# An attention-plus-MLP kernel: normalized rows transposed by DMA instead of TensorE, with output stores and v loads moved to ScalarE's DMA queue

## Chip, cores and metric

The kernel runs on one core of one Trainium2 chip. The metric is device time in microseconds (us) of one execution; three executions of the kernel before gave 367.08, 367.95 and 368.9, so the median is 367.95.

## What is computed

For 8 batches, 8 heads, 576 positions and a head width of 64 the kernel computes a causal attention whose scores carry a bias from a running sum, and then a layer norm and a two-layer MLP with a residual on the 512 values of each position:

```python
scores = scale * np.matmul(q, k.transpose(0, 1, 3, 2))
cum = np.cumsum(np.maximum(s, 0.0), axis=-1)
bias = -(cum[:, :, :, None] - cum[:, :, None, :])
scores = np.where(causal, -1e9, scores + np.minimum(bias, 0.0))
attn = softmax(scores)                      # over the last axis
x = np.matmul(attn, v).transpose(0, 2, 1, 3).reshape(8, 576, 512)
xn = (x - mu) / np.sqrt(var + 1e-06) * g_ln
out = x + np.maximum(xn @ w_ch1, 0.0) @ w_ch2
```

## The kernel before, in words

Everything is written out by hand: one Python loop over the 64 heads, `n = 8*b + h` (L745), puts instructions into each engine's queue, and each engine runs its queue in order. `pre(n)` (L675) issues what head `n` needs from GpSimd and SyncE ahead of its matmuls. `scores(b, h)` (L304) makes three PSUM banks `sa`, `sb`, `sc` of transposed scores (three buffers, `ps_s`), which ScalarE turns into `er` by Exp (L323); from head 10 on GpSimd masks the diagonal blocks of `er` (L331). `scores_d` (L341) does the last 64 by 64 corner of two heads at once, into `sd`. `pv_next()` (L729) multiplies with `v` for the head two steps back (`pot`, L389), and VectorE divides into `xb` (a batch's rows, 4 tiles of 128 positions by 512) and `xm` (the last 64 positions of two batches together).

Between these, TensorE is filled with *units* of the MLP of the batch before, taken from `queue` by `run_units`. A batch has 32 units: 16 of `mlp1` (L493: four 128x512 matmuls into `ph`, a Relu into `hT` by ScalarE, L507, or by VectorE for the first unit of a head, L505) and 16 of `mlp2` (L511: four matmuls into `py`; after each fourth unit VectorE writes `yo`, L524, and SyncE stores it, L542). `ph` and `py` share two PSUM buffers (`ps_m`). The units of batch `b-1` begin in head `8b+4`, right after its scores; its `mlp1` fills heads `8b+4` to `8b+7` and its `mlp2` the four heads after. After head 63 only units are left: the rest of batch 6, batch 7, and the mixed tiles of `xm`.

`mlp1` needs the normalized rows `xn` (VectorE, L451, without the factor `rstd`, which `yo` applies later) with the 512 features on partitions, `xT`. `ln_tr` (L478) does that: four TensorE transposes of 128x128 into PSUM `trx` (L484, buffers of `ps_t`) and one copy by VectorE or ScalarE (L100, L98). Per batch there are 4 tiles, and in every second batch a fifth for `xm`, in heads `8b+2` and `8b+3`, or at the end for batch 7.

From group 5 on (a group is four heads, `gam = n // 4`) the rows of k and q come in by SyncE (`ld_rows`, L159, six shared staging buffers with the v loads), are cast with their bias columns by GpSimd (`cast_rows`, L172, in `pre`, ahead of that head's masks) and are transposed into `kq` by SyncE's `dma_start_transpose` (`tr_rows`, L182, line L186), 6 to 2 heads before they are used. `ld_v` (L134) loads v tiles on SyncE, `cast_v` (L152) casts them on GpSimd. So SyncE's queue holds row loads, v loads, row transposes and output stores in one order, and it waits in that order. The program gives the DMAs of SyncE and ScalarE eight completion semaphores in turn, and a DMA is issued only when the one eight places before it in program order has landed.

Of the kernel before, what the change touches and what calls it, by code (L numbers as in the profile page):

```python
# [9 lines left out]
F32 = mybir.dt.float32  # L10
BF16 = mybir.dt.bfloat16
# [4 lines left out]
P = 128  # L16
# [3 lines left out]
def kernel(  # L20
# [28 lines left out]
    NPE = 5  # L49
# [46 lines left out]
    def copy_on(eng, out, in_):  # L96
        if eng == "act":
            nc.scalar.copy(out=out, in_=in_)  # L98
# [35 lines left out]
    def ld_v(b, t):  # L134
        if b >= B:
            return
        pn = P if t < NF else TL
        tmp = stage.tile([P, H, D], F32, name="vtmp", tag="st")
        nc.sync.dma_start(
            out=tmp[:pn], in_=v[b, :, t * P : t * P + pn, :].rearrange("h s d -> s h d")  # L140
        )
        loaded["v", b, t] = tmp
# [287 lines left out]

    def ln_open(b):
        mvs[b] = small.tile([P, 5, 2], F32, name="mv", tag="mv", bufs=2)
        xTs[b] = xtp.tile([P, KD, 512], BF16, name="xT", tag="xT")

    def ln_rstd(b):
        n = len(x_tiles(b))
        rs = rstd[:, b, 0:n]
        nc.vector.tensor_scalar_add(out=rs, in0=mvs[b][:, 0:n, 1], scalar1=1e-6)  # L438
        nc.gpsimd.tensor_tensor(out=rs, in0=rs, in1=mhalf[:, 0:n], op=ALU.pow)  # L439

    def ln_aggr(b, t):
# [2 lines left out]
    def ln_xn(b, t):  # L444
        tiles = x_tiles(b)
        if t >= len(tiles):
            return
        if b > 0:
            ln_aggr(b, t)
        xn = xnp.tile([P, Dm], BF16, name="xn", tag="xn")  # L450
        nc.vector.scalar_tensor_tensor(  # L451
            out=xn,
            in0=tiles[t],
            scalar=mvs[b][:, t, 0:1] if b > 0 else mean0[:, t : t + 1],
            in1=gb,
            op0=ALU.subtract,
            op1=ALU.mult,
        )
        xns[b, t] = xn
        if b > 0 and t == len(tiles) - 1:  # L460
            ln_rstd(b)

# [10 lines left out]
    def ln_first_rstd():  # L473
        for t in range(NF):
            ln_aggr(0, t)
        ln_rstd(0)

    def ln_tr(b, t, eng="dve"):  # L478
        if (b, t) not in xns:
            return  # L480
        xn = xns.pop((b, t))
        tr = ps_t.tile([P, KD, P], BF16, name="trx", tag="tr")
        for kd in range(KD):
            nc.tensor.transpose(tr[:, kd, :], xn[:, kd * P : (kd + 1) * P], ident)  # L484
        if t < NF:
            dst = xTs[b][:, :, t * P : (t + 1) * P]
        else:
            dst = xTm[:, :, (b // 2) * P : (b // 2 + 1) * P]
        copy_on(eng, dst, tr)

    first_unit = [False]

    def mlp1(xT, fb):  # L493
        on_dve = first_unit[0]
        ph = ps_m.tile([P, 512], F32, name="ph", tag="m")
        for kd in range(KD):
            nc.tensor.matmul(  # L497
                ph,
                lhsT=w1_bf[:, kd, fb * P : (fb + 1) * P],
                rhs=xT[:, kd, :],  # L500
                start=(kd == 0),
                stop=(kd == KD - 1),
            )
        if on_dve:
            nc.vector.tensor_scalar_max(out=hT[:, fb, :], in0=ph, scalar1=0.0)  # L505
        else:
            nc.scalar.activation(out=hT[:, fb, :], in_=ph, func=ACT.Relu)  # L507
# [31 lines left out]
    def batch_units(b):  # L539
        def of_t(t):  # L540
            def put(yo, c0, c1):
                nc.sync.dma_start(out=out[b, t * P : (t + 1) * P, c0:c1], in_=yo)  # L542
            return xb[b][:, t, :], rstd[:, b, t : t + 1], put
        return chunk_units(lambda: xTs[b], of_t)

# [7 lines left out]

    queue = []
    pend = []

    def run_units(n, dve_first=False):
# [117 lines left out]
    def pre(n):  # L675
        if n == 0:
            nc.vector.memset(mhalf, -0.5)
            ld_cast_pair(4)
        elif n == 1:
            ld_w1(1)  # L680
        elif n == 3:
            ld_cast_pair(5)
            for t in range(NT):
                ld_cast_v(1, t)
        elif n == 4:
            ld_w1(2)
            ld_w1(3)
        elif n == 7:
            ld_cast_pair(6)
            ld_w2(0)  # L690
            ld_cast_pair(7)
            ld_w2(1)
        elif n == 10:
            ld_w2(2)
            ld_w2(3)
        elif n == 12:
            nc.vector.memset(cT[:, :, 0, :, 0], -1.0)
            nc.vector.memset(cT[:, :, 1, :, 1:4], 1.0)
        elif n == 14:
            for r in rows:  # L700
                nc.gpsimd.memset(r[:, :, :, KA:P], 0.0)
        if n in PAIR_LOADS:
            ld_cast_pair(PAIR_LOADS[n])
        if n % 4 == 0 and 2 <= n // 4 + 1 < NPE:
            aug(n // 4 + 1, nc.sync)
        for gam in range(NPE, NG):
            m = n - 4 * gam
            if m == -6:
                ld_rows(gam, 0), ld_rows(gam, 1)
            elif m == -5:  # L710
                cast_rows(gam, 0), cast_rows(gam, 1)
                ld_rows(gam, 2), ld_rows(gam, 3)
            elif m == -4:
                tr_rows(gam, 0), tr_rows(gam, 1)
                cast_rows(gam, 2), cast_rows(gam, 3)
                ld_rows(gam, 4)
            elif m == -3:
                tr_rows(gam, 2), tr_rows(gam, 3)
                cast_rows(gam, 4)
            elif m == -2:  # L720
                tr_rows(gam, 4)
        for nb in range(2, B):
            m = n - H * nb + (5 if nb == 2 else 7)
            if 0 <= m < NT:
                ld_v(nb, m)
            if 1 <= m <= NT:
                cast_v(nb, m - 1, "pool")

# [16 lines left out]
    for n in range(BH):  # L745
# [25 lines left out]
        if n == 8:  # L771
# [6 lines left out]
            def columns(t):  # L778
                cols = slice(t * P, (t + 1) * P)
                for fb, ph in enumerate(phs):  # L780
                    for kd in range(KD):
                        nc.tensor.matmul(
                            ph[:, cols],
                            lhsT=w1_bf[:, kd, fb * P : (fb + 1) * P],
                            rhs=xTs[0][:, kd, cols],
                            start=(kd == 0),
                            stop=(kd == KD - 1),
                        )
# [33 lines left out]
        lt = {2: (0, 1), 3: (2, 3, 4)}.get(h, ()) if b > 1 else ()  # L822
        for t in lt:
            ln_tr(b - 1, t, "act" if b == 2 else "dve")
            if t != 1 and t != 4:
                run_units(1)
                nu -= 1
# [48 lines left out]
```

The softmax here doesn't subtract the row's maximum and nothing guards it: scores larger than these inputs give would overflow.

## Time and profile before

| what | value |
|---|---|
| median of three runs | 367.95 us |
| the profiled execution | 368.54 us, of which 366.8 us from the first to the last instruction |
| TensorE matmuls | 355.0 us busy |
| VectorE, ScalarE, GpSimd | 202.9, 191.3, 164.9 us busy |
| `mlp1` and `mlp2` matmuls (L497, L515) | 116.4 and 132.1 us busy |
| transposes of `xn` (L484) | 144, 13.8 us busy |
| DMA between 80 and 270 us | mean share of the 16 engines 0.86, 176 GB/s |
| SyncE's queue | 32 stores of 256 KB, 30 v loads, 110 row loads, 55 transposes |
| granted TensorE clock | 0.998 |

Busy time of TensorE is the union of matmul durations, which overlap in the pipeline: a 128x512 matmul has a duration of 379 ns, but one starts every 216 ns. What a matmul costs the stream is therefore the distance between starts, not the duration. A few matmul records are missing, so a group of four may show three. In the profile `SPq` and `ACTq` are the queues of SyncE and ScalarE in which DMAs are issued; the time given for a DMA there is that of its issue[...], not of the transfer.

### The profile page before, as it was taken

To read this page: it belongs to the slowest core of one execution; us is meant where nothing else is said; L and a number is where in the kernel's file an instruction comes from. 1 tells how busy PE (TensorE), PEld (TensorE's weight loads), DVE (VectorE), ACT (ScalarE), POOL (GpSimd) and SP (SyncE) were. 2 spreads that over 40 slices of the span, in tenths; PEclk is the share of its full clock that TensorE was granted. 3 is DMA by queue.
4 is the path that set the end of the run, shared out by engine and by line. 5 is a ranking of instruction groups with operands and counts; after the bars stand their busy time and mean duration, and the time that the engine had idled before them with its cause. 6 is when DMAs were issued, how large, how long until landed. Compare 5 with 4: busy or idle time off the path is not lost.

```text
span 366.8 us, 8315 instructions
## 1 busy us (share of the span) xinstructions
PE 355.0 (97%) x3017; PEld 197.1 (54%) x3067; DVE 202.9 (55%) x535; ACT 191.3 (52%) x367; POOL 164.9 (45%) x447
## 2 busy tenths in 40 slices
PE   8998999999999999999999999999999999999995
PEld 3677555565555555555455555555555554444444
DVE  7697789684357554944384547743675483112211
ACT  5895988467732673367534753476337522501410
POOL 8854468667633656344675563554852101000000
PEclk9999999999999999999999999999999999999999
DMA  8999999999965999599979986798830011011013
GB/s 144 162 195 178 202 211 193 163 240 176 183 146 141 206 199 181 104 215 163 188 176 213 194 183 140 189 191 182 174 102 2 0 59 57 1 58 59 0 31 86
DMA packets 156653, 52.17 MB, mean 142 GB/s; under 512 B 143641, under 2 KB 151940, under 8 KB 156612
## 3 DMA queue, kind: packets, MB, share of 16 engines
q1 hardware_dynamic: 138868, 43.08, 55.5%
q0 software_dynamic: 17344, 8.03, 18.9%
q8 instruction: 24, 0.39, 0.5%
q10 hardware_dynamic: 400, 0.52, 0.4%
q14 instruction: 17, 0.14, 0.2%
HBM read 37.11 MB, written 9.44 MB: 127 GB/s over the span
## 4 chain that ended last, share of the span: by engine, by line
PE 72%; DVE 7%; DMA 6%; SPq 4%; POOL 4%; issue 3%; ACT 3%; POOLq 0%; ACTq 0%
PE py L515 26%; PE ph L497 25%; PE pot L389 6%; SPq L164 3%; PE sc L312 3%; PE sa L312 3%; PE sb L312 3%; DMA rowtmp<-in_q_dram 2%; PE idle L568 2%; DMA vtmp<-in_v_dram 2%; DVE xn L451 2%; PE trx L484 2%; DVE stats L423 1%; POOL er L331 1%; ACT er L323 1%
## 5 line engine op out<-in xcount | busy, mean ns | idle before, releaser
L515 PE MATMUL py<-w_bf,hT 128*128 128x512 bf16 (+1 forms) x565 | 132.1, 373 | 1.6 <-DVE yo L524 0.4
L497 PE MATMUL ph<-xT,w_bf 128*128 128x512 bf16 x478 | 116.4, 379 | 1.1 <-DVE yo L524 0.2
L507 ACT ACTIVATE hT<-ph 128x512 bf16<-128x512 f32 x102 | 61.0, 598 | 64.4 <-PE ph L497 64.4
L515 PEld LDWEIGHTS <-hT 128*128 128x128 bf16 x592 | 53.5, 98 | 49.1 <-issue 0.9
L497 PEld LDWEIGHTS <-w_bf 128*128 128x128 bf16 x560 | 50.1, 97 | 51.3 <-issue 2.9
L323 ACT ACTIVATE er<-sa 128x512 bf16<-128x512 f32 x64 | 38.2, 597 | 70.9 <-PE sa L312 50.1
L331 POOL TENSOR_SCALAR_AFFINE_SELECT er<-er 128x128 bf16<-128x128 bf16 x216 | 59.7, 300 | 22.5 <-ACT er L323 22.3
L505 DVE TENSOR_SCALAR hT<-ph 128x512 bf16<-128x512 f32 x38 | 26.3, 692 | 56.7 <-PE ph L497 49.0
L176 POOL CAST rows<-rowtmp 128x512 bf16<-128x512 f32 (+1 forms) x55 | 33.5, 609 | 50.7 <-DMA rowtmp<-in_q_dram 46.0
L312 PEld LDWEIGHTS <-kq 68*128 68x128 bf16 x452 | 33.4, 97 | 27.4 <-issue 1.7
L389 PEld LDWEIGHTS <-er 128*128 128x128 bf16 x960 | 37.5, 98 | 14.9 <-issue 0.7
L389 PE MATMUL pot<-v_bf,er 128*128 128x65 bf16 x960 | 40.2, 193 | 0.5 <-PE sd L355 0.3
L397 DVE RECIPROCAL rinv<-pot 128x5 f32<-128x5 f32 x64 | 12.3, 192 | 49.2 <-PE pot L389 48.9
L323 ACT ACTIVATE er<-sc 128x512 bf16<-128x512 f32 x64 | 39.2, 612 | 0.0
L323 ACT ACTIVATE er<-sb 128x512 bf16<-128x512 f32 x64 | 38.4, 599 | 0.3 <-PE sb L312 0.2
L524 DVE SCALAR_TENSOR_TENSOR yo<-py,rstd,xb 128x512 f32<-128x512 f32 x32 | 23.9, 748 | 26.2 <-PE py L515 19.7
L399 DVE TENSOR_TENSOR xb<-pot,rinv 128x256 f32<-128x256 f32 x64 | 27.2, 425 | 2.2
L102 POOL CAST v_bf<-vtmp 128x512 bf16<-128x512 f32 (+1 forms) x30 | 18.5, 617 | 19.6 <-DMA vtmp<-in_v_dram 19.5
L439 POOL TENSOR_TENSOR rstd<-rstd,mhalf 128x4 f32<-128x4 f32 (+1 forms) x8 | 8.8, 1095 | 38.0 <-DVE rstd L438 37.9
L312 PE MATMUL sc<-kq 68*128 68x256 bf16 (+1 forms) x216 | 25.3, 229 | 0.3
L423 DVE BATCH_NORM_STATS2 stats<-xb 128x6 f32<-128x128 f32 (+2 forms) x100 | 25.3, 313 | 0.4
L312 PE MATMUL sb<-kq 68*128 68x64 bf16 (+1 forms) x172 | 24.5, 244 | 0.9 <-DMA kq<-rows 0.6
(101 smaller groups left out, 322.1 us busy)
## 6 DMA issues: line engine op xcount, KB each, us to landing
out_dram<-yo SPq DMA_DIRECT2D x32, 256.0 KB
vtmp<-in_v_dram SPq DMA_DIRECT2D x24, 256.0 KB
rowtmp<-in_k_dram SPq DMA_DIRECT2D x44, 128.0 KB
rowtmp<-in_q_dram SPq DMA_DIRECT2D x44, 128.0 KB
w_bf<-in_moe_w_ch_dram POOLq DMA_DIRECT2D x8, 512.0 KB, 10.7
kp<-in_k_dram POOLq DMA_DIRECT2D x9, 144.0 KB, 6.8
qp<-in_q_dram POOLq DMA_DIRECT2D x9, 144.0 KB, 7.0
v_bf<-in_v_dram POOLq DMA_DIRECT2D x8, 128.0 KB, 8.1
```

The costliest lines, as they stand in the source:

```text
L176: nc.gpsimd.tensor_copy(out=r[0:pn, :, :, 0:D], in_=loaded.pop(("rows", gam, t))[0:pn])
L312: nc.tensor.matmul(a[:, c + a0 - q0 : c + a1 - q0], lhsT=k_cols(b, h, kb), rhs=cols, start=True, stop=not (pe_mask and diag),)
L323: nc.scalar.activation(out=e[:, o : o + 512], in_=a, func=ACT.Exp, scale=scale)
L331: nc.gpsimd.affine_select(out=e[:, o : o + P], in_=e[:, o : o + P], compare_op=ALU.is_ge, fill=0.0, base=0, pattern=[[1, P]], channel_mult ...
L389: nc.tensor.matmul(pot[:, t, :], lhsT=e[:, o : o + P], rhs=vv[:, kb, h, :], start=(kb == 0), stop=(kb == last),)
L399: nc.vector.tensor_tensor(out=xb[b][:, :, hs], in0=pot[:, 0:NF, 0:D], in1=rinv[:, 0:NF].unsqueeze(2).to_broadcast([P, NF, D]), op=ALU.mult,)
L423: nc.vector.bn_stats(out=st[b][:, t, part, :], in_=x[:, lo:hi])
L497: nc.tensor.matmul(ph, lhsT=w1_bf[:, kd, fb * P : (fb + 1) * P], rhs=xT[:, kd, :], start=(kd == 0), stop=(kd == KD - 1),)
L505: nc.vector.tensor_scalar_max(out=hT[:, fb, :], in0=ph, scalar1=0.0)
L507: nc.scalar.activation(out=hT[:, fb, :], in_=ph, func=ACT.Relu)
L515: nc.tensor.matmul(py[0], lhsT=hT[:, fb, t * P : (t + 1) * P], rhs=w2_bf[:, fb, c0:c1], start=(fb == 0), stop=(fb == FB - 1),)
L524: nc.vector.scalar_tensor_tensor(out=yo, in0=py[0], scalar=rs, in1=x[:, c0:c1], op0=ALU.mult, op1=ALU.add)
```

## The change

The transposes of batches 1 to 7 leave TensorE. `xn` tiles are now written in pairs (`[P, 2, Dm]`), and `ln_dma` transposes a pair (128 x 1024) straight into `xT` with one SyncE DMA; the `xm` tile goes alone. `xT` and `xTm` get the layout tile, feature block, position, so that a matmul reads four pieces of 128 columns. Batch 0 keeps `ln_tr`. In `pre`, the two DMAs come in heads `8b+2` (for batch 1: one in head 18, one in head 19, after that head's row loads), the one for `xm` in head `8b+4`; for batch 7 they follow the last units of batch 6's queue.

v loads go from SyncE to ScalarE (queued after the head's Exps), with three staging buffers of their own; rows keep four. Stores go from SyncE to ScalarE and are issued five units after the `yo` that they store. GpSimd's casts of rows and v move from `pre` to `post`, which runs after the head's scores, masks and first unit; its power for `rstd` moves from the batch's layer norm to the end of head `8b+3`. The transposes of k and q tile 4 move ahead of the head's other work on SyncE.

```diff
@@ tiles
-    stage = ctx.enter_context(tc.tile_pool(name="stage", bufs=6))
+    stage = ctx.enter_context(tc.tile_pool(name="stage", bufs=4))
-    xnp = ctx.enter_context(tc.tile_pool(name="xnp", bufs=5))
+    xnp = ctx.enter_context(tc.tile_pool(name="xnp", bufs=3))
-    xTm = const.tile([P, KD, 512], BF16, name="xTm")
+    xTm = const.tile([P, NF, KD, P], BF16, name="xTm")
@@ ld_v
-        tmp = stage.tile([P, H, D], F32, name="vtmp", tag="st")
-        nc.sync.dma_start(
+        tmp = stage.tile([P, H, D], F32, name="vtmp", tag="v", bufs=3)
+        nc.scalar.dma_start(
@@ layer norm
+    def ln_dma(b, j):
+        if j == 2 and b % 2 == 0:
+            return
+        xn = xns.pop((b, j))
+        if j < 2:
+            nc.sync.dma_start_transpose(
+                out=xTs[b][:, 2 * j : 2 * j + 2].rearrange("p t k s -> p (t k) s"),
+                in_=xn.rearrange("p t d -> p (t d)"),
+            )
+        else:
+            nc.sync.dma_start_transpose(out=xTm[:, b // 2], in_=xn[:, 0, :])
@@ mlp1
-                rhs=xT[:, kd, :],
+                rhs=xT[:, :, kd, :],
@@ batch_units
-                nc.sync.dma_start(out=out[b, t * P : (t + 1) * P, c0:c1], in_=yo)
+                stores.append([5, out[b, t * P : (t + 1) * P, c0:c1], yo])
@@ run_units
+                for x in stores:
+                    x[0] -= 1
                 queue.pop(0)()
+                while stores and stores[0][0] == 0:
+                    _, dst, src = stores.pop(0)
+                    nc.scalar.dma_start(out=dst, in_=src)
@@ pre
+        for gam in range(NPE, NG):
+            m = n - 4 * gam
+            if m == -2:
+                tr_rows(gam, 4)
...
+        if n == 18 or n == 19:
+            ln_dma(1, n - 18)
+        elif n > 19 and n % H == 2:
+            ln_dma(n // H - 1, 0), ln_dma(n // H - 1, 1)
+        if n > 19 and n % H == 4:
+            ln_dma(n // H - 1, 2)
+
+    def post(n):
+        for gam in range(NPE, NG):
+            m = n - 4 * gam
+            if m == -5:
+                cast_rows(gam, 0), cast_rows(gam, 1)
+            elif m == -4:
+                cast_rows(gam, 2), cast_rows(gam, 3)
+            elif m == -3:
                 cast_rows(gam, 4)
@@ head loop
         scores(b, h)
+        for nb in range(2, B):
+            m = n - H * nb + (5 if nb == 2 else 7)
+            if 0 <= m < NT:
+                ld_v(nb, m)
         run_units(1, True)
         if h % 2 == 0:
             scores_d(b, h // 2)
+        post(n)
         run_units(1)
...
-        lt = {2: (0, 1), 3: (2, 3, 4)}.get(h, ()) if b > 1 else ()
-        for t in lt:
-            ln_tr(b - 1, t, "act" if b == 2 else "dve")
...
         if b > 1 and h == 3:
+            ln_pow(b - 1)
             run_units(len(queue))
             queue += batch_units(b - 1)
@@ tail
         run_units(1)
-        ln_tr(B - 1, t, "act")
+        if t % 2 == 1 or t == NF:
+            ln_dma(B - 1, t // 2)
+    ln_pow(B - 1)
```

More of the change, by code (lines that the diff above doesn't have):

```diff
@@ L432, in ln_open @@
         mvs[b] = small.tile([P, 5, 2], F32, name="mv", tag="mv", bufs=2)
-        xTs[b] = xtp.tile([P, KD, 512], BF16, name="xT", tag="xT")
+        xTs[b] = xtp.tile([P, NF, KD, P], BF16, name="xT", tag="xT")
     def ln_rstd(b):
@@ L438, in ln_rstd, with ln_pow @@
         nc.vector.tensor_scalar_add(out=rs, in0=mvs[b][:, 0:n, 1], scalar1=1e-6)
+    def ln_pow(b):
+        n = len(x_tiles(b))
+        rs = rstd[:, b, 0:n]
         nc.gpsimd.tensor_tensor(out=rs, in0=rs, in1=mhalf[:, 0:n], op=ALU.pow)
@@ L449, in ln_xn @@
             ln_aggr(b, t)
-        xn = xnp.tile([P, Dm], BF16, name="xn", tag="xn")
+        if t % 2 == 0:
+            xns[b, t // 2] = xnp.tile([P, 2, Dm], BF16, name="xn", tag="xn")
+        xn = xns[b, t // 2][:, t % 2, :]
         nc.vector.scalar_tensor_tensor(
@@ L458, in ln_xn @@
         )
-        xns[b, t] = xn
         if b > 0 and t == len(tiles) - 1:
@@ L476, in ln_first_rstd, with ln_tr @@
         ln_rstd(0)
[L478 to L481, printed above, removed]
+        ln_pow(0)
+    def ln_tr(b, t, eng):
+        xn = xns[b, t // 2][:, t % 2, :]
         tr = ps_t.tile([P, KD, P], BF16, name="trx", tag="tr")
@@ L484, in ln_tr @@
             nc.tensor.transpose(tr[:, kd, :], xn[:, kd * P : (kd + 1) * P], ident)
-        if t < NF:
-            dst = xTs[b][:, :, t * P : (t + 1) * P]
-        else:
-            dst = xTm[:, :, (b // 2) * P : (b // 2 + 1) * P]
-        copy_on(eng, dst, tr)
+        copy_on(eng, xTs[b][:, t], tr)
+    def ln_dma(b, j):
[7 more added lines that the diff above has]
+            )
+        else:
+            nc.sync.dma_start_transpose(out=xTm[:, b // 2], in_=xn[:, 0, :])
     first_unit = [False]
@@ L555 @@
     pend = []
+    stores = []
     def run_units(n, dve_first=False):
@@ L710, in pre @@
             elif m == -5:
-                cast_rows(gam, 0), cast_rows(gam, 1)
                 ld_rows(gam, 2), ld_rows(gam, 3)
@@ L714, in pre @@
                 tr_rows(gam, 0), tr_rows(gam, 1)
-                cast_rows(gam, 2), cast_rows(gam, 3)
                 ld_rows(gam, 4)
@@ L718, in pre @@
                 tr_rows(gam, 2), tr_rows(gam, 3)
+        if n == 18 or n == 19:
[12 more added lines that the diff above has]
+            elif m == -3:
                 cast_rows(gam, 4)
-            elif m == -2:
-                tr_rows(gam, 4)
         for nb in range(2, B):
             m = n - H * nb + (5 if nb == 2 else 7)
-            if 0 <= m < NT:
-                ld_v(nb, m)
             if 1 <= m <= NT:
@@ L784, in columns @@
                             lhsT=w1_bf[:, kd, fb * P : (fb + 1) * P],
-                            rhs=xTs[0][:, kd, cols],
+                            rhs=xTs[0][:, t, kd, :],
                             start=(kd == 0),
@@ L821 @@
         pend.append((b, h))
-        lt = {2: (0, 1), 3: (2, 3, 4)}.get(h, ()) if b > 1 else ()
-        for t in lt:
-            ln_tr(b - 1, t, "act" if b == 2 else "dve")
-            if t != 1 and t != 4:
-                run_units(1)
-                nu -= 1
         if n == 2 * H + 2:
```

## The prediction

> **What bounds the kernel now.** I read the page's busy rows first, then TensorE's own instructions, then the queues that the change loads.
>
> ```profile
> PE 355.0 (97%) x3017; PEld 197.1 (54%) x3067; DVE 202.9 (55%) x535; ACT 191.3 (52%) x367; POOL 164.9 (45%) x447
> ...
> PE   8998999999999999999999999999999999999995
> ...
> ACT  5895988467732673367534753476337522501410
> ...
> DMA  8999999999965999599979986798830011011013
> ```
>
> TensorE is full in every slice, so what leaves its stream shortens the kernel unless a wait takes its place. The DMA row is nearly as full until slice 29. ScalarE is free on average, but its slices 4 and 5 (37 to 55 us) are full.
>
> The timeline of TensorE at head 19's end gives the price of a transpose:
>
> ```profile
> 75.97 0.39 PE L484 MATMUL trx<-ident,xn 128*128 128x128 bf16 x4
> 76.20 0.38 PE L312 MATMUL sa<-kq 68*128 68x512 bf16 x1
> ...
> 80.13 0.61 PE L484 MATMUL trx<-ident,xn 128*128 128x128 bf16 x8
> 80.58 0.38 PE L312 MATMUL sa<-kq 68*128 68x512 bf16 x1
> ...
> 81.24 1.03 PE L497 MATMUL ph<-xT,w_bf 128*128 128x512 bf16 x4
> ```
>
> Four transposes occupy 76.20 - 75.97 = 0.23 us (0.2235 over the groups with all records). L497 at 81.24 is the first `mlp1` of batch 1, right behind the last transposes: here `xT` is needed at once.
>
> Issue prices, min/median/max in ns, from the tiles `vtmp`, `yo` and `kq`:
>
> ```profile
> L139 SPq DMA_DIRECT2D vtmp<-in_v_dram x30: 440/590/1761, 29.4 to 248.4; - x30
> ```
> ```profile
> L542 SPq DMA_DIRECT2D out_dram<-yo x32: 332/364/1099, 66.6 to 335.6; - x32
> L549 SPq DMA_DIRECT2D out_dram<-yo x5: 466/468/569, 353.4 to 363.5; - x5
> L550 ACTq DMA_DIRECT2D out_dram<-yo x5: 498/498/577, 353.4 to 363.5; - x5
> ```
> ```profile
> L186 SPq DMA_TRANSPOSE kq<-rows x55: 1215/1260/2791, 61.2 to 267.5; - x55
> ```
>
> SyncE's own waits show that its stores held the loads behind them:
>
> ```profile
> SPq L542 <- DVE yo L524: 41.7, 12, 17.5
> ```
>
> **What the skill says.** The Trainium skill, "TensorE: Matmul & The Clock Gate", section "Wait — 56ns, not 53.3ns?": warm starts are 55.6 ns apart at 128 columns and 215.7 at 512; the trace agrees (0.2235/4 = 55.9 ns; 216 ns). "Advanced Engine Details and Errata", section "X-Bar Transpose (TRN2)": such DMAs are as fast as plain ones; the trace agrees, 256-byte packets of both kinds have a median of 18 ns. "DMA: Bandwidth & Descriptors", section "Issuing engines are not separate DMA queues": DMAs of several engines share the 16 DMA engines, so a second issuer saves only issue time. The trace has one instance, the paired stores at 353.4 us: both issues took 0.57 us, where SyncE alone needs 0.33.
>
> **Removed.** 7 batches x 4 tiles + 4 `xm` tiles = 32 groups x 0.2235 = 7.15 us of TensorE, on the path. VectorE's and ScalarE's copies (22 and 10, 0.42 and 0.59 us) go too; VectorE is at 55%, so they are worth nothing by themselves. The new `xT` layout costs nothing: `sa` reads its queries as one run in early heads and as four pieces in later ones, 376 to 390 ns in both.
>
> **Transposes, batch 1 (the largest new cost).** The second pair waits for this VectorE instruction, and on SyncE for the row loads of head 19:
>
> ```profile
> 77.98 0.75 DVE L451 SCALAR_TENSOR_TENSOR xn<-xb,mv,gb 128x512 bf16<-128x512 f32 x1
> ```
>
> It ends at 78.73; nothing before it on VectorE is removed. SyncE gets there as follows. Casts now come behind masks, so the cast of q/k tile 4 of group 5 (head 17: masks end near 71, tile landed near 71.8) ends near 72.7. Then: its transpose 1.26, four loads 2.2, first pair 1.26, four loads 2.2: 79.65. The transposes of the trace land 2.7 us after issue into empty rings (113.22 to 115.94, from the completion events) and 4.5 behind a train of loads; I take 3.8: 83.5. TensorE would want it at 81.24 less the five groups gone, 5 x 0.2235: 80.1. Stall 3.4, say 3.3 us; bounds 2 (lands 82.1) and 5 (ring crowded, or clock lost after a long pause). A gain is excluded: VectorE's end plus 2.7 is 81.4, already past 80.1.
>
> **Batches 2 to 6: hidden.** In batch 2 the last `xn` of the second pair ends at 112.0; by the same addition SyncE is past its loads at 110.5 and first pair at 111.8, issues at 112.0, lands by 115.4 to 117; need 118.96 - 0.9 = 118.1. Cover: 1 to 2.7 us, made of head 27 and its units. Once it is gone, each lost us costs five. **Batch 7:** `xn` tile 3 ends 301.45, rings empty, lands 304.3; four units of batch 6 reach to 306.44 - 1.1 = 305.3. Hidden.
>
> **v loads on ScalarE, heads 11 to 15.** Here ScalarE has no room:
>
> ```profile
> 55.93 0.62 ACT L507 ACTIVATE hT<-ph 128x512 bf16<-128x512 f32 x1
> 56.40 1.62 ACT L98 COPY kq<-trqk 64x576 bf16<-64x576 bf16 x2
> 58.05 0.60 ACT L323 ACTIVATE er<-sa 128x512 bf16<-128x512 f32 x1
> ```
>
> TensorE already waits 0.40 us at 58.08 for that copy. Four loads at 0.59 (SyncE's row for the same transfer) before head 15's copies, less 0.75 us of ScalarE's gaps in heads 12 and 13: 4 x 0.6 - 0.75 = 1.65 us. Bounds: 0.9 (at the minimum, 440 ns) and 3.5 (1.06 each).
>
> **v load and store ahead of the Relu, heads 8b+4 and 8b+5.**
>
> ```profile
> 120.22 0.27 ACT L358 ACTIVATE er<-sd 64x128 bf16<-64x128 f32 x1
> 120.95 0.60 ACT L507 ACTIVATE hT<-ph 128x512 bf16<-128x512 f32 x1 [0.46 <-PE ph L497]
> ```
>
> Head 28: Exps end at 120.36; then v load 0.6, store 0.43 (between 364 and 498), `sd`'s Exp 0.27, Relu 0.6: 122.26. The fourth unit needs that `ph` buffer near 122.01: late by 0.25. Head 29 has no `sd`: level. Four batches (28, 36, 44, 52) make 1.0 us; bounds 0 and 8 (below). In the other heads ScalarE issues during `mlp2`, where no Relu waits. The semaphore eight places back costs nothing: in head 27 the v load wants the first pair (landed about 115) and gets there at 115.5.
>
> **Other moves at nothing.** Casts behind masks: `kq` tile 4 still lands about 110.4 for scores at 118.3; cover, SyncE freed of its 41.7 us of store waits. Stores five units late: `yo` has three buffers, reused 12 units later, about 7 units after the issue, against 2 us to land. `rstd`'s power: wanted first by `yo`, 16 units on.
>
> **Sum.** -7.15 + 3.3 + 1.65 + 1.0 = -1.2 us on the profiled 368.54 (span 366.8 and 1.7 around it). The median of the runs is 0.6 below that execution: 367.95 - 1.2 = 366.8.
>
> **Rivals.** *(a) Nearly cancelled*, the sum, 364.5 to 369.2 as the small terms vary: chance 0.40. *(b) The gain goes through*: batch 1's stall at 2 or less and ScalarE's issues at their minima, -7.15 + 1.5 + 0.9 + 0 = -4.7: 363.2. For it: SyncE loses its store waits. Against: VectorE's 78.73. 0.18. *(c) Slower: ScalarE's issues stretch* beside SyncE's transposes, which keep that queue issuing most of the time. With p for load plus store, heads 8b+4 lose p - 0.78 and heads 8b+5 lose p - 1.05, four times each. The gain left by the first two costs, 2.2 us, is gone from 8p - 7.32 = 2.2: p = 1.19 against my 1.03. At 0.9 and 0.6: 4.7 there, 2.85 in heads 11 to 15, so +3.7: 371.7; at 1.1 and 0.7, 375. For it: the pair at 353.4, slowed by 0.24. Against: 128 KB stores are all it shows. 0.30. *(d) DMA becomes the bound*: 176 GB/s x 190 us = 33.4 MB; six batches add 3.5 MB; over 184 us that is 201 GB/s, where the best slices sustain 200 to 215. If only 190 hold, 194 us, 4 more than now in that stretch: 371.9. 0.12.
>
> About 0.5%, 1.8 us, is what a measurement can tell. (a) splits 0.12 faster, 0.26 same, 0.02 slower; (b) is faster; (c) 0.03 same, 0.27 slower; (d) 0.01 and 0.11. Together 0.30, 0.30, 0.40. Range 361.8 (b with batch 1 nearly hidden) to 376 (c's far end); (a) alone 364.5 to 369.2.
>
> **What would show it.** TensorE has 128 fewer matmuls; a gap of 2 to 5 us near 80 us before L511's `ph` (the old L497), released by the transpose; a wait of about 1 us more near 58 to 61 us on ScalarE's copies; gaps of a few tenths in heads 28, 36, 44, 52; none at 118 or 305. ScalarE's issue rows decide between (a) and (c): medians near 0.6 and 0.43, or near 1. I am wrong if batch 1's pair lands before 81, or if gaps appear in every head.

## The result and the profile after

The changed kernel takes 383.21 us (median of four runs, 382.65 to 386.35) against 367.82 of the kernel before on the same chip: a ratio of 1.043, 95% interval 1.037 to 1.050. It is slower by 15 us, and lies beyond the range that was forecast. The profiled execution has a span of 380.6 us, 13.8 above before. In what follows medians are over all runs of a kernel, and ratios leave out slow runs, those more than 1.5% above the fastest of the same kernel.

The page of the changed kernel, its row of busy times and four rows of its 40 slices (9.5 us each):

```profile
PE 353.9 (93%) x2939; PEld 191.5 (50%) x2939; DVE 196.3 (52%) x513; ACT 185.7 (49%) x357; POOL 167.9 (44%) x447
...
PE   8999998945999899988999799889999999999995
...
ACT  5895997330753376336733474356535611411510
...
PEclk9999999995999999999999899999999999999999
DMA  7999995999868996999679957999761004001013
```

TensorE's row, nearly all nines before, now has a hole in slices 8 and 9 (counted from 0; 76 to 95 us) and dents in slices 13, 17, 18, 22, 25 and 26. The clock row (`PEclk`, the clock granted to TensorE, in tenths) dips in slices 9 and 22: behind these two gaps the matmuls run slower, too. The work that left TensorE did shorten its stream; waits took its place.

TensorE at the hole (start, duration, instruction, and in brackets the idle time and what ended it):

```profile
80.05 0.39 PE L312 MATMUL sc<-kq 68*128 68x256 bf16 x4
89.71 1.86 PE L511 MATMUL ph<-xT,w_bf 128*128 128x512 bf16 x4 [9.28 <-DMA xT<-xn]
```

This is batch 1's first `mlp1` (L511 now), waiting for the second transposed pair, and TensorE does nothing meanwhile. The dents in slices 13, 18, 22 and 26 end with something else, a Relu of ScalarE. First TensorE, then ScalarE with its queue, in head 28:

```profile
131.21 1.03 PE L511 MATMUL ph<-xT,w_bf 128*128 128x512 bf16 x4
133.77 1.02 PE L511 MATMUL ph<-xT,w_bf 128*128 128x512 bf16 x4 [1.53 <-ACT hT L521]
```
```profile
129.40 0.61 ACT L323 ACTIVATE er<-sc 128x512 bf16<-128x512 f32 x1
131.21 0.44 ACTq L139 DMA_DIRECT2D vtmp<-in_v_dram  x1
132.55 0.36 ACTq L583 DMA_DIRECT2D out_dram<-yo  x1
132.96 0.27 ACT L358 ACTIVATE er<-sd 64x128 bf16<-64x128 f32 x1 [2.95 <-DMA rowtmp<-in_q_dram]
133.14 1.06 ACT L521 ACTIVATE hT<-ph 128x512 bf16<-128x512 f32 x2
```

The Exp of `sc` ends at 130.01. The v load's issue takes 0.44 us, but it starts 1.20 us later; the store's takes 0.36 and starts 0.91 us after the v load's. What ends these waits is in the completion events: a k row load of SyncE, issued at 126.52, lands at 131.13, and ScalarE's v load, which has the same semaphore, goes out 0.08 us after; a q row load lands at 132.48, and the store goes out 0.08 after. Only then come `sd`'s Exp and the Relus, so the fourth unit finds no free `ph`. At the Exp the profile names an unrelated row load as what ended 2.95 us of idle time: the Exp does not read those rows, it stands behind a DMA that shares the row load's semaphore.

Where the span's 13.8 us come from, by how far each head's first matmul moved against before. A gap in this table and below is the time from one start of a matmul to the next, 0.2 to 0.4 us more than the idle time in brackets:

| place | us |
|---|---|
| transposes gone from TensorE | -7.15 |
| head 20, gap of 9.47, and the lower clock behind it | +11.5 |
| heads 28, 37, 44, 52: gaps of 1.91, 1.59, 2.50, 1.69 behind ScalarE's waits, and clock | +8.8 |
| heads 35 and 51: VectorE's five `xn` ahead of `yo`, in part covered by transposes before | +1.7 |
| heads 40 and 41: waits of before for late kq rows that are gone | -1.55 |
| heads 11 to 15 | +0.25 |

They add up to 13.55; TensorE's last matmul starts 13.5 us later than before. After this the theory was: two separate costs. Batch 1's pair is late because SyncE gets to it late and because it lands slowly; and ScalarE's DMAs wait for SyncE's DMAs, eight places back in the common order of semaphores, with Relus queued behind. The rival for the second was that ScalarE's issues, or the bytes in the rings, delay the Relus.

### The profile page after: what moved, and what is told of

The parts are those of the page before. It is cut to its first block, busy times and chain, and to the rows that moved or that the text cites. A ratio compares the mean times of both kernels' runs of the same rounds, so it can differ in the third digit from the quotient of the medians.

```text
span 380.6 us, 8141 instructions
## 1 busy us (share of the span) xinstructions
PE 353.9 (93%) x2939; PEld 191.5 (50%) x2939; DVE 196.3 (52%) x513; ACT 185.7 (49%) x357; POOL 167.9 (44%) x447
## 4 chain that ended last, share of the span: by engine, by line
PE 67%; DMA 10%; DVE 10%; ACT 4%; issue 3%; POOL 3%; SPq 3%; ACTq 1%; POOLq 0%
PE ph L511 28%; PE py L529 23%; PE pot L389 5%; DMA rowtmp<-in_q_dram 4%; PE sc L312 3%; DVE xn L458 3%; PE sb L312 2%; SPq L164 2%; PE sa L312 2%; DMA v_bf<-in_v_dram 2%; DVE stats L423 2%; ACT er L323 2%; DMA xT<-xn 2%; DVE xb L399 1%; DMA vtmp<-in_v_dram 1%
## 5 line engine op out<-in xcount | busy, mean ns | idle before, releaser
L511 PE MATMUL ph<-xT,w_bf 128*128 128x512 bf16 x496 | 121.4, 386 | 15.7 <-DMA xT<-xn 9.3
L529 PE MATMUL py<-w_bf,hT 128*128 128x512 bf16 (+1 forms) x592 | 134.0, 373 | 2.1 <-DVE yo L538 2.1
L331 POOL TENSOR_SCALAR_AFFINE_SELECT er<-er 128x128 bf16<-128x128 bf16 x216 | 64.1, 309 | 102.5 <-ACT er L323 102.0
L511 PEld LDWEIGHTS <-w_bf 128*128 128x128 bf16 x560 | 50.7, 98 | 69.6 <-issue 19.2
L389 PEld LDWEIGHTS <-er 128*128 128x128 bf16 x960 | 37.9, 98 | 14.5 <-issue 1.2
L312 PE MATMUL sa<-kq 68*128 68x512 bf16 x64 | 24.6, 384 | 0.8 <-DMA kq<-c 0.7
L458 DVE SCALAR_TENSOR_TENSOR xn<-xb,mv,gb 128x512 bf16<-128x512 f32 x28 | 23.3, 832 | 1.0
```

Source lines behind the costliest of these rows:

```text
L312: nc.tensor.matmul(a[:, c + a0 - q0 : c + a1 - q0], lhsT=k_cols(b, h, kb), rhs=cols, start=True, stop=not (pe_mask and diag),)
L331: nc.gpsimd.affine_select(out=e[:, o : o + P], in_=e[:, o : o + P], compare_op=ALU.is_ge, fill=0.0, base=0, pattern=[[1, P]], channel_mult ...
L389: nc.tensor.matmul(pot[:, t, :], lhsT=e[:, o : o + P], rhs=vv[:, kb, h, :], start=(kb == 0), stop=(kb == last),)
L458: nc.vector.scalar_tensor_tensor(out=xn, in0=tiles[t], scalar=mvs[b][:, t, 0:1] if b > 0 else mean0[:, t : t + 1], in1=gb, op0=ALU.subtrac ...
L511: nc.tensor.matmul(ph, lhsT=w1_bf[:, kd, fb * P : (fb + 1) * P], rhs=xT[:, :, kd, :], start=(kd == 0), stop=(kd == KD - 1),)
L529: nc.tensor.matmul(py[0], lhsT=hT[:, fb, t * P : (t + 1) * P], rhs=w2_bf[:, fb, c0:c1], start=(fb == 0), stop=(fb == FB - 1),)
```

## The experiments

Line numbers of each profile are those of its own kernel.

**One repair at a time.** Batch 1 back on TensorE, everything else as changed:

```diff
+        lt = {18: (0, 1), 19: (2, 3, 4)}.get(n, ())
+        for t in lt:
+            ln_tr(1, t, "act")
...
-        if n == 18 or n == 19:
-            ln_dma(1, n - 18)
```

> The changed kernel with batch 1's five tiles transposed on TensorE and copied by ScalarE, as in the kernel before; batches 2 to 7 still by DMA. The changed kernel lost 9.5 us in one gap before batch 1's first MLP matmul and about 2 us more after it, at a lower clock. Theory 'late pair in head 19': that loss goes and five groups of 0.22 us come back, so about 383.2 - 11.5 + 1.1 = 373, and the gaps of 1.3 to 2.5 us in heads 28, 35, 37, 44, 51 and 52 stay as they are. Rival 'the DMA engines have too little room for any added transposes': the head 20 gap is only moved, the rows of the next group come late instead, and the time stays above 378.

Measured: 375.5 us (ratio 1.022, 1.019 to 1.025), 2.5 above the theory's figure and below the rival's. Head 20's gap went; the other four stayed (one of them in head 36 in place of 37), and four of 1.0 to 1.25 us came up in heads 18 to 21. Three of these end with a copy or a Relu of ScalarE, behind a DMA that had waited for its semaphore (heads 19 and 21) or taken 2.10 us to issue (head 20); the one in head 18 ends with VectorE's `yo`.

v loads and stores back on SyncE, everything else as changed:

```diff
-        nc.scalar.dma_start(
+        nc.sync.dma_start(
             out=tmp[:pn], in_=v[b, ...]
...
-                    nc.scalar.dma_start(out=dst, in_=src)
+                    nc.sync.dma_start(out=dst, in_=src)
```

> The changed kernel with v loads and the five-units-late stores issued by SyncE again; ScalarE issues nothing until the mixed tiles. Theory 'completion semaphores': ScalarE's issues wait for SyncE's row loads eight places back, and hold the Relu behind them; then the gaps of 1.6 to 2.5 us in heads 28, 37, 44 and 52 and the clock lost after one of them go, about 8 us: 375, with the head 20 gap left at 9 us or a little longer. Rival 'volume': the gaps come from 245 GB/s being the most that the DMA engines give, and stay, since the bytes are the same: 383 or more.

Measured: 374.38 us (1.019, 1.016 to 1.022), as the theory had it. The gaps behind ScalarE in heads 28, 37 and 52 went, and of head 44's 1.7 us were left, behind a `yo` that waited. Head 20's gap shrank to 6.24 us as well, which was not expected. SyncE's queue, first as changed, then in this run:

```profile
78.01 2.90 SPq L498 DMA_TRANSPOSE xT<-xn  x1
80.95 0.58 SPq L164 DMA_DIRECT2D rowtmp<-in_k_dram  x1
...
82.74 0.66 SPq L164 DMA_DIRECT2D rowtmp<-in_q_dram  x1
83.50 2.30 SPq L498 DMA_TRANSPOSE xT<-xn  x1
```
```profile
77.89 1.24 SPq L498 DMA_TRANSPOSE xT<-xn  x1
79.17 0.58 SPq L139 DMA_DIRECT2D vtmp<-in_v_dram  x1
...
83.20 1.26 SPq L498 DMA_TRANSPOSE xT<-xn  x1
```

The issue of a pair takes 1.24 to 1.26 us here and 2.30 to 2.90 in the changed kernel, where ScalarE's v load, and for the first pair its store, were still under way. The second pair still goes out only 0.3 us earlier, since the v load and the store now stand ahead of it; what shortened the gap is its landing, 3.48 us after the issue instead of 6.18.

**One part alone, on the kernel before.** v loads and late stores on ScalarE, no DMA transposes of `xn`:

```diff
-        nc.sync.dma_start(
+        nc.scalar.dma_start(
             out=tmp[:pn], in_=v[b, ...]
...
+                while stores and stores[0][0] == 0:
+                    _, dst, src = stores.pop(0)
+                    nc.scalar.dma_start(out=dst, in_=src)
```

> The kernel before with v loads (own three buffers, rows four) and five-units-late stores on ScalarE, nothing else: TensorE still transposes, casts stay ahead of the masks. Prediction's step: 1.65 us lost in heads 11 to 15 and 1.0 in heads 8b+4, so 370.6. Theory 'completion semaphores': without the added transposes rows land sooner, so waits in heads 28, 37, 44, 52 are under 1 us each and the time lies between 368 and 371. If the issues by themselves hold the Relu (case (c) of the prediction) the time is 372 to 375.

Measured: 382.74 us (1.042, 1.036 to 1.047). The expectation was far too low: this part alone costs as much as the whole change. Its waits of TensorE:

```profile
PE ph L497 <- ACT hT L507: 11.3, 9, 3.1
```

11.3 us in nine waits for Relus (total, times, longest); two stretches of 3.41 us at half the clock, behind gaps in heads 21 and 37, cost another 3.4 us. Ahead of the waits ScalarE's DMAs follow the landing of a SyncE row transpose: the v load at 91.54, 0.08 us after the transpose issued at 87.74 had landed. The DMA transposes of `xn` are not needed for this cost.

Fifteen transposes of a constant tile on SyncE at the places of `ln_dma`, which nobody reads, and TensorE's transposes kept:

```diff
+    def extra(j, k=2 * KD):
+        nc.sync.dma_start_transpose(out=ddst[j][:, 0:k], in_=dsrc[:, 0 : k * P])
```

> The kernel before plus 15 DMA transposes on SyncE at the places where the changed kernel has them (heads 18, 19, 20 and 8b+2, 8b+4), from a constant tile into tiles that nobody reads; batch 7's are left out. It prices the added DMA volume and issue time alone, without a wait for VectorE and with nothing moved to ScalarE. Theory 'late pair' and 'completion semaphores': hidden, 368 to 370. Rival 'volume': rows and v come late, 373 or more, with TensorE waits on the row transposes.

Measured: 379.35 us (1.032, 1.026 to 1.038), well above the theory's figure, on the rival's side. TensorE has gaps in heads 39, 48 and 55, together 5.5 us; the rest of the loss lies in smaller waits and a stretch of half clock. Among its waits:

```profile
PE pot L391 <- POOL er L333: 3.9, 4, 2.4
```

That is `pv` waiting for masks, 3.9 us in four waits: GpSimd's casts stand ahead of the masks and wait for row loads. The same kernel with the casts behind the masks should then be rid of it:

```diff
-                cast_rows(gam, 0), cast_rows(gam, 1)
...
+    def post(n):
+                cast_rows(gam, 0), cast_rows(gam, 1)
```

> The kernel before with fifteen transposes of a constant tile on SyncE, as in the run before, and GpSimd's casts moved behind the masks. Theory (the idle transposes cost time only because casts ahead of the masks wait for row loads behind them): gaps at pot and sb in heads 39, 48 and 55 go, 367 to 370. Rival (the transposes take DMA time or SyncE time that anything behind them needs): stays at 377 to 380.

Measured: 382.02 us (1.040, 1.038 to 1.042). The waits for masks went, as foreseen, but the time did not:

```profile
176.67 1.67 PE L499 MATMUL ph<-xT,w_bf 128*128 128x512 bf16 x7
181.02 0.38 PE L314 MATMUL sa<-kq 68*128 68x512 bf16 x1 [2.67 <-issue]
182.50 0.61 PE L314 MATMUL sb<-kq 68*128 68x64 bf16 x3 [1.11 <-DMA kq<-rows]
```

The rows of k and q themselves now come late, in heads 24, 32, 40, 48 and 56. My theory of this cost fell: the casts decide who waits, not whether. Fifteen transposes among SyncE's old queue cost about 12 us, and 14.5 with the casts moved; which part of the old order makes them dear was not separated, so this stays open.

**Is it the semaphore?** The first attempt wrote the row and pair DMAs of a head into the program after its first unit:

```diff
         if h % 2 == 0:
             scores_d(b, h // 2)
+        sync_rows(n)
         post(n)
```

> The changed kernel with one difference: the row loads, row transposes and xn transposes of a head are written into the program after that head's first unit, instead of ahead of its scores. The order on each engine stays as it was (SyncE's queue, ScalarE's queue); what changes is which DMA stands eight places ahead of a ScalarE DMA in program order: the v load of head 28 then follows a transpose of head 26 instead of a row load of head 27. Theory (ScalarE waits for the landing of a SyncE DMA eight places back, and its Relus wait behind): the gaps of TensorE in heads 28, 37, 44 and 52 (1.9, 1.6, 2.5, 1.7 us) go, with the clock lost after them: 374 to 377. Rival (ScalarE's issue time, or full DMA rings, delay the Relus): nothing changes, 383. In both, head 20's gap stays near 9 us. A third possibility: SyncE in its turn waits for v loads, and row tiles come late: above 383, gaps at sb or pot.

Measured: 387.05 us (four runs, 381.23 to 393.88, too wide for a ratio), the gaps in the heads where the changed kernel has them. But it decides nothing: all 67 DMAs of ScalarE and all 216 of SyncE had the same semaphore as before the edit, so the wait was still there. The order in which the semaphores are dealt, called program order above, is therefore not that of the source.

The second attempt asked the opposite: issues without waits. It uses a kernel with the repairs made so far (below), and has ScalarE issue two 128-byte DMAs in each of ten heads with Relus:

```diff
+    def small_dma(n, j):
+        if 20 <= n < 56 and n % H in (4, 5):
+            j += 2 * (n % 2)
+            nc.scalar.dma_start(out=tiny[j], in_=zeros[0:1, 0:64])
```

> The repaired kernel with DMAs of 128 bytes issued by ScalarE, two in each of heads 20, 21, 28, 29, 36, 37, 44, 45, 52, 53, where the changed kernel has its v load and store. They move nothing to speak of and wait for no data. Theory (ScalarE's wait for a SyncE DMA that is still under way, by the shared completion semaphores, is the cost): gaps of 1 to 2.5 us before the Relus of most of these heads, 5 to 12 us above the repaired kernel, and each such DMA is issued 0.08 us after a SyncE DMA has landed. Rival (the issue itself, or the v loads' and stores' bytes): 20 x 0.35 us of ScalarE time, at most 2 us above it.

Measured: 366.48 us (0.998, 0.996 to 1.000), where the repaired kernel takes 365.59. The expectation of my theory was missed, for a reason that helps it. From the end of ScalarE's last instruction to each DMA I added up the idle time: 0.8 us in all here, 18.1 us before the 41 DMAs of the changed kernel between 80 and 270 us. (5.6 of these 18.1 us fall into or just ahead of head 20's gap.) So the semaphores were free this time:

```profile
L701 ACTq DMA_DIRECT2D tiny<-zeros x20: 504/540/1548, 82.0 to 239.6; - x20
```

20 issues at a median of 540 ns (the middle number) are 12.9 us in sum, two in a row in front of a Relu each time, and they cost about 1 us, of the size of the runs' spread. For 5.3 of the 12.9 us ScalarE was still at work on earlier instructions. Issue time alone does not explain 8.8. The same small DMAs in heads 8b+1 and 8b+2, where units are `mlp2`:

> As the run with 128-byte DMAs in the heads with Relus, but in heads 8b+1 and 8b+2, where the units are mlp2 and no Relu waits behind ScalarE. Theory (only a Relu behind the wait costs): within 1 us of the repaired kernel. Rival (the Exps behind the wait cost as much): as much above it as the other run.

Measured: 366.71 us (0.998, 0.995 to 1.001), 1.1 above the repaired kernel, with intervals that overlap. Here ScalarE did wait before them, 7.2 us in all and once 3.06. The gaps of TensorE over 0.7 us in this profile from head 20 on (2.87 us in head 52 the longest) end with landings of `xT` or `kq`, none with ScalarE.

The third attempt took the waits away where Relus stand and nowhere else: the changed kernel, with only the v loads and stores of heads 8b+4 and 8b+5 on SyncE.

```diff
+    def dma_eng():
+        return nc.sync if busy[0] else nc.scalar
...
+        busy[0] = n >= 20 and h in (4, 5)
         pre(n)
```

> The changed kernel, with the v loads and stores of heads 8b+4 and 8b+5 (from head 20 on) on SyncE and all others on ScalarE as in the change. Theory (a ScalarE wait for a semaphore costs where Relus stand behind it, and nothing in the heads with mlp2): the gaps of heads 28, 36/37, 44 and 52 (7.7 us and some clock) go, although ScalarE still waits for semaphores in the other heads: 374 to 376, as with all of them on SyncE (374.4). Rival (ScalarE's waits cost in every head, or the gaps come from full DMA rings): 378 to 383. In both, head 20's gap stays at 6 to 9 us.

Measured: 373.17 us (1.012, 1.006 to 1.019). ScalarE from the end of head 27 into head 28 now:

```profile
126.48 0.41 ACTq L144 DMA_DIRECT2D vtmp<-in_v_dram  x1
126.99 0.59 ACTq L588 DMA_DIRECT2D out_dram<-yo  x1
...
128.68 0.61 ACT L328 ACTIVATE er<-sc 128x512 bf16<-128x512 f32 x1
129.16 0.27 ACT L363 ACTIVATE er<-sd 64x128 bf16<-64x128 f32 x1
129.89 0.60 ACT L526 ACTIVATE hT<-ph 128x512 bf16<-128x512 f32 x1 [0.46 <-PE ph L516]
```

The first two issues are head 27's, whose units are `mlp2`. In head 28 no wait stands between the Exps and the Relu, which again waits for TensorE. All four gaps are gone, and the time falls by 10 us, of which 1.3 come from head 20's gap (8.15 us here). ScalarE was still idle for 7.6 us before its other DMAs: 1.84 us of it in that gap, 1.77 before the load at 126.48 and 2.43 in head 43, both for semaphores, and TensorE has no gap at those two. The bytes are the same, and the small DMAs have priced the issues; together the two runs leave the wait as the cause. A kernel in which ScalarE's DMAs have semaphores of their own, the direct test, was not run.

**Batch 1, and what can be had.** The changed kernel with the second pair ahead of head 19's row loads:

```diff
+        if n == 19:
+            ln_dma(1, 1)
         for gam in range(NPE, NG):
```

> The changed kernel with batch 1's second pair ahead of head 19's four row loads in SyncE's queue. Theory (the row loads ahead of it, each waiting for a landing eight places back, cost 2.55 us of the gap, and their traffic lengthens the landing from 3.8 to 6.2): issue at 80.95, landing 84.7 to 87, gap of 4.5 to 7 us in place of 9.5, 377 to 380. Rival (the landing is slow for another reason and the place in the queue is irrelevant): gap over 8 us, 382 to 384.

Measured: head 20's gap is 6.27 us, so the order on SyncE made up 3.2 of the 9.47. (In the changed kernel the row loads ahead of the pair go out within 0.1 us of one another: they take issue time, 2.6 us, and do not wait.) The kernel took 385.84 us (1.050, 1.048 to 1.052) all the same: gaps in heads 28 to 52 grew, and its first heads began 2 us later.

Both repairs together, DMAs on SyncE and batch 1 on TensorE:

> The changed kernel with v loads and stores on SyncE and batch 1's five tiles transposed by TensorE. If the two costs (ScalarE's waits, batch 1's wait) are separate and add up: 374.4 - 8.2 (head 20's step there) + 5 x 0.2235 = 367.3. If a repair only hands the time to the next wait, as in the run with batch 1 on TensorE alone, where four gaps of about 1 us came up in heads 18 to 21: 369 to 371.

Measured: 366.74 us (0.999, 0.997 to 1.001). They add up as worked out, and bring the change to no difference. Of what was left, two gaps of 1.7 and 2.3 us in heads 28 and 44 came from the late stores. VectorE there:

```profile
119.76 0.75 DVE L538 SCALAR_TENSOR_TENSOR yo<-py,rstd,xb 128x512 f32<-128x512 f32 x1 [3.04 <-DMA out_dram<-yo]
```

`yo` waits 3.04 us for the store of the `yo` three before, which stood behind two transposes in SyncE's queue. Two more edits were made, a fourth `yo` buffer and the fifth `xn` of batches 3 and 5 one head later:

```diff
-    yop = ctx.enter_context(tc.tile_pool(name="yop", bufs=3))
+    yop = ctx.enter_context(tc.tile_pool(name="yop", bufs=4))
...
+        elif b > 2 and h == 2:
+            ln_xn(b - 1, NF)
```

> The run with v loads and stores on SyncE and batch 1 on TensorE (366.7), with two repairs: a fourth yo buffer (in heads 28 and 44 there, yo waits for the store of the yo three before it: gaps of 1.7 and 2.3 us), and the fifth xn of batches 3 and 5 one head later (heads 35 and 51: 1.25 us each, behind VectorE's five xn). If each gap goes and nothing comes up behind it: 366.7 - 4.0 - 1.5 (clock after head 44's gap) - 2.0 = 359 to 361, faster than the kernel before. If the gaps return elsewhere: 364 to 367.

Measured: 365.59 us (0.994, 0.993 to 0.996). The four gaps went, but a good part of the gain came back: its profile (367.35 us, its runs spread from 362.75 to 369.43) shows late kq rows at head 40, gaps of 1.42 and 2.08 us, and half the clock for 6.8 us around them:

```profile
174.35 0.39 PE L312 MATMUL sa<-kq 68*128 68x512 bf16 x1 [1.04 <-DMA kq<-rows]
176.43 0.61 PE L312 MATMUL sb<-kq 68*128 68x64 bf16 x3 [1.69 <-DMA kq<-rows]
```

With batch 1 on DMA as well, its second pair ahead of the loads:

> As the repaired kernel, but batch 1 transposed by DMA too, its second pair ahead of head 19's row loads. Of head 20's gap of 9.5 us, leaving ScalarE's DMAs out took 3.2 (6.24) and the order on SyncE took 3.2 (6.27). If both add: gap of 3 us, at most 1 us of clock, less the 1.1 of TensorE's transposes: 2 to 3 us above the repaired kernel. If they are the same time counted twice: gap near 6, 6 to 8 us above it.

Measured: 372.33 us (1.015, 1.010 to 1.019), 6.7 above the repaired kernel. Head 20's gap is 3.81: the pair is issued at 79.96 and lands 3.77 later. The gap follows the first expectation, the time the second. Behind the gap TensorE runs at half the clock until 88.7, which costs 2.5 us where at most 1 was allowed for; late kq rows in heads 40, 55 and 56 take 4.9 us, only 1.4 more than in the repaired kernel's own profile.

Two edits that take something off SyncE ahead of those rows: the transposes of `xm` two heads later, alone, and together with the v loads of heads 8b+1 to 8b+3 on ScalarE, where no Relu waits.

```diff
-        if n > 23 and n % H == 4:
+        if n > 23 and n % H == 6:
             ln_dma(n // H - 1, 2)
...
+        v_eng[0] = nc.scalar if n > 24 and h in (1, 2, 3) else nc.sync
```

> The repaired kernel with only the transposes of xm (1.24 us of SyncE each) two heads later, where SyncE has no row transposes due at once. If they alone made the rows of head 40 late: 362.5 to 364.5. If the rows are late for the whole queue's sake: 365 to 366, and the gap moves to another head.

Measured: 365.88 us (0.994, 0.990 to 0.997), no different from the repaired kernel: gaps in head 40 for kq rows (1.16 us) and in heads 44 and 52 for `xT` (1.49 and 2.16).

> The repaired kernel (365.6) with the v loads of heads 8b+1 to 8b+3 on ScalarE (from batch 3 on) and the transposes of xm two heads later, so that SyncE has 1.9 us of issues less ahead of the row transposes of heads 8b+2 to 8b+4. If late kq rows (head 40's gap of 2.1 and head 39's of 1.4 us in its profile) are what is left, they go: 362 to 364. If ScalarE's v loads wait for semaphores and hold Exps, as much comes back: 366 or more.

Measured: 362.27 us (0.982, 0.976 to 0.987), faster than the kernel before by 1.8%, and 3.6 us below the run with only the transposes of `xm` moved. Its page:

```profile
PE 350.7 (97%) x2959; PEld 191.1 (53%) x2959; DVE 196.0 (54%) x513; ACT 188.8 (52%) x362; POOL 171.1 (47%) x447
...
PE   8899999999999999999999999999999999999995
...
PEclk9999999999999999999999999999999999999999
DMA  7999999399999989999899999999850024011013
```

TensorE's row is whole again. 27 of the 32 groups left it, 27 x 0.2235 = 6.0 us, and its last matmul begins 6.2 us earlier than before. ScalarE still waits 4.9 us before its 12 DMAs from 80 to 270 us, without a gap on TensorE.

## Why the prediction was wrong, by its own steps

The sum said -1.2 us; TensorE's last matmul came 13.5 us later than before. The terms that were off make up the 14.7 us between: ScalarE's waits +7.8 (8.8 for 1.0), batch 1 +8.2 (11.5 for 3.3), heads 35 and 51 +1.7 (not in the sum), heads 11 to 15 -1.4, and heads 40 and 41 -1.55 (waits of before that the prediction did not see).

**"The semaphore eight places back costs nothing": the step that failed.** I tested one place, head 27, with SyncE's times of before (pair landed about 115, wanted at 115.5). In the changed kernel SyncE runs later and its DMAs land later: medians from 80 to 270 us of 5.25 us for a pair and 4.41 for a v load, where SyncE alone (the run with all of them on SyncE) needs 3.05 and 3.34. Eight places back is then often still under way: 21 of ScalarE's 41 DMAs there went out within 0.1 us of such a landing, 19 of them behind a DMA of SyncE. In head 27 itself the v load waited 1.00 us for the pair. So "v load and store ahead of the Relu" was put at 1.0 us, with 8 as its far end, and measured 8.8.

**Batch 1, 3.3 us with 5 as bound: measured 11.5, mis-sized.** The path was right (second pair, SyncE, `xT`), two terms were not. Its issue was worked out as 79.65 and came at 83.50: the transpose of tile 4 began 1.0 us later than worked out and its issue took 1.92 us instead of 1.26, the first pair's took 2.90 instead of 1.26, and the eight row loads took 5.0 instead of 4.4. Its landing was taken as 3.8 and took 6.18. A third was only hinted at, the clock: about 2 us. With the pair ahead of the loads and no DMA on ScalarE, batch 1 on DMA had 79.96, 3.77 and a gap of 3.81, close to the sum's 79.65, 3.8 and 3.4. The landing is the one that the sum took; the issue meets the sum's by luck, for the sum had four row loads (2.2 us) ahead of the pair and this run has a v load and a store. I priced a busy pair of queues with the rows of a single one.

**Removed, -7.15 us: right** in size, and not all of it usable. It was put "on the path", but in heads 35 and 51 the path runs through VectorE, where `yo` stands behind five `xn`. Of the 0.84 us that came back in each of them, 0.45 is the two groups of the head before, which had covered that wait; the rest is that the five `xn` with the work between them take 4.88 us instead of 4.48. Why one of the five, written in pairs now, takes 1.08 us instead of 0.75 was not looked into.

**Issue prices: right.** The changed kernel's rows for its v loads and stores:

```profile
L139 ACTq DMA_DIRECT2D vtmp<-in_v_dram x30: 374/428/724, 47.1 to 255.6; - x30
L583 ACTq DMA_DIRECT2D out_dram<-yo x32: 338/363/1287, 72.3 to 352.1; - x32
```

Together 0.79 us, under the 1.03 assumed and far under the 1.19 from which rival (c) decided. That rival had the side, was 8 us short in time at its far end (375), and did not have the mechanism: ScalarE's issues did not stretch, they waited. The prediction said that issue medians would decide between (a) and (c); by them (a) would have won. It had no line that looked at the time before the issue. The place it named, heads 28, 36, 44 and 52, was right but for 37.

**Heads 11 to 15, 1.65 us: too much,** 0.25. **Batches 2 to 7 hidden: right,** no TensorE gap behind `xT` in any, but in batch 2 by luck: its second pair landed at 128.91, and its first `mlp1` began at 128.96, a cover of 0.05 us where 1 to 2.7 was forecast. **Rival (d), DMA as the bound: wrong** at this size: the best kernel moved 200 GB/s from 80 to 270 us with TensorE busy for 188.7 of the 190 us. The late kq rows look like its sign, but went when 1.9 us of issues were taken off SyncE.

The Trainium skill's "DMA: Bandwidth & Descriptors", section "Issuing engines are not separate DMA queues", says that a second issuer only saves issue time. I read this as "it costs nothing else". It saved time indeed (428 ns for a v load, 590 on SyncE), but SyncE's issues of pairs grew from a median of 1.25 us (all DMAs on SyncE) to 1.95, and ScalarE paid with its waits.

## What to carry to other kernels

Before a DMA is put on an engine that also computes, ask what that engine waits for before it may issue, completion semaphores shared with the other queue included, and which consumer is queued behind; put it where the next instruction of that engine has slack. Test such a wait with the other queue's times after the change, not before it. When transposes leave TensorE, look for the stalls that they had covered, and keep on TensorE those whose result is needed at once.

## What the runs showed of the hardware that was not expected

- Pairs issue and land more slowly while ScalarE's v loads and stores are under way beside the row loads: SyncE's issues of pairs have a median of 1.95 us in the changed kernel, 2.17 where ScalarE's DMAs were left out of two heads in eight, and 1.25 and 1.24 in two kernels without them; they land after 5.25 us against 3.05. ScalarE's issuing by itself is not enough: with two of its 128-byte DMAs issued 0.4 to 1.5 us ahead, pairs still took 1.23 and 1.26 us. That points to the 256 KB transfers, but no run varied their size alone. Transposes of rows kept their median of 1.26. DMA moved more, not less, just then. The changed kernel in the gap and behind it (length, busy times of PE, PEld, DVE, ACT, POOL with instructions, then clock, DMA share, which adds up packets and can pass 1, and GB/s):

```profile
80.00:90.00 10.00, 0.72 (x8) 0.46 (x6) 1.38 (x5) 1.57 (x3) 4.47 (x11) 0.69 1.29 245
90.00:94.00 4.00, 4.00 (x25) 1.98 (x24) 0.69 (x1) 0.84 (x2) 1.94 (x6) 0.50 1.06 170
94.00:100.00 6.00, 6.00 (x50) 3.19 (x48) 2.66 (x9) 3.63 (x8) 2.73 (x8) 1.00 0.82 157
213.50:216.90 3.40, 3.40 (x15) 1.50 (x13) 0.42 (x1) 2.06 (x4) 2.60 (x9) 0.50 1.14 264
```

- The clock after a gap is 0.5 or 1.0 here, nothing between, and 0.5 comes in stretches of 3.41 us or a small multiple of it: 10.24 us in and behind head 20's gap, of which TensorE was busy for 4.3 (about 2 us lost), 3.41 us behind the 2.50 us gap of head 44 (1.7 us lost), and 6.83 us in the repaired kernel. The Trainium skill's "TensorE: Matmul & The Clock Gate", section "Why this matters for your kernels", advises against idle gaps of more than about 3 us; here 2.50 was enough. But a gap of 2.48 us (head 28 with batch 1 on TensorE) and one of 2.87 (head 52 with the small DMAs in `mlp2` heads) cost no clock. In the traces each stretch starts a whole number of 3.41 us after the last change of the clock, so where a gap falls on that grid may decide; no run tested it.
- An issue does not stop what ScalarE already has in hand: of the 20.0 us of issues of its 41 DMAs from 80 to 270 us, 8.9 us lie under instructions of ScalarE that stood ahead of them. The prediction had added issues and instructions one behind another.
